# An mLSTM cell and a gated unit on one core: the order of Up's 64-row and 128-row products

## The chip, the cores and the metric

The kernel runs on one core of a Trainium2 chip. The time is the device time of one execution in microseconds (us); lower is better. A core has five engines with an instruction queue each: PE (TensorE, the matrix products; PEld is its loading of weights), DVE (VectorE), ACT (ScalarE), POOL (GpSimd) and SP (SyncE, which here only issues DMAs). They run side by side and wait for one another by semaphores.

## The reference, cut to what matters

Two blocks follow one another. The first is an mLSTM cell (4 batches, 8 heads, 768 steps, head dimension 40) that gives `attn_out`; the second is a gated unit with an input width of 320 and an inner width of 2048.

```python
x = attn_out.transpose(0, 2, 1, 3).reshape(B * S, H * D)   # 3072 x 320
h = x @ w_in                                               # "Up":   320 -> 2048
g = h * np.cos(h)                                          # the gate
out = g @ w_out                                            # "Down": 2048 -> 320
```

All values are float32. The recurrence of the first block is computed in chunks of steps, with one exponent matrix per head and chunk.

## The kernel before, in words

**Tiling.** The 768 steps are cut into 6 chunks of 128 (`NC`). A chunk of one batch is a *cell*, numbered n = 4 x chunk + batch, 24 in all. The tokens of one chunk, 4 batches x 128 steps = 512, are the moving columns of Up. The contraction of Up has 320 rows: two blocks of 128 (`NK`) and a rest of 64. The inner width 2048 is 16 blocks of 128, taken two at a time, e = 0 and 1, so a chunk has 8 pairs f2 = 0..7.

**Order.** The program is written out by hand; every engine executes its instructions in the order in which they are issued. `first_cells` does chunk 0 of the mLSTM block. Then `both_parts(c, b)` runs for every chunk c and every b in 0..3; it does the gated unit for chunk c, beside the cell n = 4(c + 1) + b of the chunk after it. In the last chunk (c = 5) no cell is left. Each `both_parts` has two half periods, i = 0 and i = 1, with one Up each, f2 = 2b + i.

**One Up** (class `Up`, L624 to L658) takes two PSUM banks from a pool of two (tag `up`), one for each e, and so needs both banks of the Up before to be free. Its constructor issues six products on PE: four with 128 rows (L636; block 0 for e = 0 and 1, then block 1 for both) and two with 64 rows (L639). In the last two, e = 0 uses rows 0 to 63 of the weights `w_in_l` and of x, and e = 1 uses rows 64 to 127, where a second copy of the same 64 rows of x stands. Each product of float32 appears in the trace as two records, two passes over the same 512 columns.

The chain behind it, for each e: `near` (L644, ACT) rounds h + 0.25 to an integer, `rest` (L647, DVE) takes the difference, `sin` (L652, ACT) is the sine of 2 pi times it, `gate` (L656, DVE) multiplies by h and writes g. `gate` is the last reader of the PSUM bank, so the next Up's first product into that bank waits for it.

**Around it on PE.** In half period i = 0 PE runs Up, `scores` (L482, 40 rows), Down's products, `values` (L508 to L517, 16 or 32 columns of weights), and in chunks 1 to 3 `seam` (L597, 40 columns of weights). In half period i = 1 it runs Up and then Down's products. From chunk 1 on, Down's products are those of a Strassen-like scheme (`products`, L717, and `run`, L743): from `sums` (L697, on DVE and POOL) of the g's, 12 or 14 per pair of blocks, handed out by `down_slot` (L786). At f2 = 1 of chunks 2 to 5 its place is taken by `late_products` of the chunk before (L737), followed by `combine_late`. `combine` (L755) adds the parts of the finished chunk on DVE and ACT after f2 = 0.

**Around it on the other engines**, in half period i = 1 of a cell: on ACT, two `near`, then two DMA issues of `seam_out` (L604, the 64 last rows of the next chunk's x, which wait for POOL's L538), then two `sin`; on DVE two `rest`, then `state` (L619, chunks 1 to 3 after POOL's `fade` L580), two `gate`, and the sums. `turn_blocks` (L455) makes the next cell's q and k on DVE, for `scores`. The 64 rows of x that Up's chunk c reads were written in chunk c - 1. At (chunk 1, f2 = 0) POOL also runs `weight_sums` (L692 to L695).

The calls of `both_parts` that matter here:

```python
for i in range(2):
    f2 = 2 * b + i
    up = Up(c, f2)
    ...
    for e in range(2):
        up.near(e)
    for e in range(2):
        up.rest(e)
    ...
    down_slot(c, f2)
```

Of the kernel before, what the change touches and what calls it, by code (L numbers as in the profile page):

```python
# [29 lines left out]
def kernel(  # L30
# [20 lines left out]
    nc = tc.nc  # L51
# [12 lines left out]
    NK = DM // 128  # L64
# [62 lines left out]
    w_in_sb = wp.tile([128, NK, DFF], FP, name="w_in_sb")  # L127

    w_in_l = wp.tile([128, NF // 2, 128], FP, name="w_in_l")
# [12 lines left out]
    def to_float32(dst, bits):  # L142
        take_apart(dst, bits)
        put_together(dst, bits)
# [166 lines left out]
    def sigmoid(c, bs=slice(0, B)):  # L311
        if c == 0:
            o = sig[c][:, bs]
            nc.scalar.activation(out=o, in_=o, func=AF.Sigmoid)
            return
        sig[c] = og
        K = C // 32
        nc.scalar.activation(out=sig[c][:, :, 0:2 * K], in_=raw_o[c][:, :, :, 0:32], func=AF.Sigmoid)
        for g in range(2):
            nc.scalar.activation(out=sig[c][:, :, 2 * K:3 * K, 16 * g:16 * g + 16:2],  # L320
                                 in_=raw_o[c][:, :, ts(g, K), 32:D], func=AF.Sigmoid)
# [7 lines left out]
    def load_two(n, which="qkKv"):  # L329
        c, b = divmod(n, B)  # L330
        m = n // 2 % 2
        for name, src in (("q", q), ("k", k)):
            if name in which:
                src = src.rearrange("b (p j) (c t a) d -> j c t (b p) (a d)", j=2, a=C // 32, t=32)
                for j in range(2):
                    for low in range(1 if n < 2 * B else 2):
                        x = 0 if low else 32
                        dst = raws[name][m][64 * j + 32 * low:64 * j + 32 * low + 32, x:x + WR]
                        nc.sync.dma_start(out=dst.rearrange("t (p x) -> t p x", x=C // 32 * D),
                                          in_=src[j, c, :, 4 * b:4 * b + 8])  # L340
        for name, dst, src in (("K", ks2[m], k), ("v", vs2[m], v)):
            if name in which:
                src = src.rearrange("b h (c t) d -> c t b h d", t=C)
                nc.sync.dma_start(out=dst[:, :, :, 0:D], in_=src[c, :, b:b + 2])
# [34 lines left out]
    def psum_o():  # L379
        return ps_o.tile([128, HP, C], FP, name="pm", tag="o")  # L380
# [6 lines left out]
    def decay_exponents(n):  # L387
        E = Es[n]
        if n < B:
            nc.vector.tensor_tensor(out=E, in0=E, in1=cols(n, 0, C), op=OP.subtract)  # L390
        nc.gpsimd.affine_select(out=E, in_=E, compare_op=OP.is_ge, fill=1.0e30, base=0,  # L391
                                pattern=[[0, H], [1, C]], channel_multiplier=-1)
# [45 lines left out]
    def clear_low():  # L438
        for w in "qk":
            nc.gpsimd.memset(raws[w][1], 0.0)  # L440
# [34 lines left out]
    def scores(n):  # L475
        pool, tag = psum(n)
        qT, kT = qkT[n]
        ps = [pool.tile([128, HP, C], FP, name="ps", tag=tag) for _ in range(2)]
        for p in range(HP):
            for j in range(2):  # L480
                r = slice(64 * j, 64 * j + D)
                nc.tensor.matmul(ps[j][:, p], kT[r, p], qT[r, p], start=True, stop=True)  # L482
        pss[n] = ps

    def weigh(n):
        for j in range(2):
            w = Es[n].rearrange("p (a j) t -> p a j t", j=2)[:, :, j]
            nc.vector.tensor_tensor(out=w, in0=pss[n][j], in1=w, op=OP.mult)  # L488
# [71 lines left out]
    def halves(n):  # L560
        for j in range(2):
            r = slice(64 * j, 64 * j + D)
            for lo, hi, x in ((0, 32, HP * 32 * j), (32, DV, H * 32)):
                s = st[n % B][r, x:x + HP * 32].rearrange("q (p d) -> q p d", p=HP)
                yield j, r, s if lo == 0 else s[:, :, 16 * j:16 * j + 16], slice(lo, hi)
# [58 lines left out]
    class Up:  # L624


        def __init__(self, c, f2):
            self.c, self.f2 = c, f2
            self.pu = [ps_u.tile([128, B * C], FP, name="pup", tag="up") for _ in range(2)]

            def x(i, r=slice(0, 128)):
                return xT[c][r, i].rearrange("p b t -> p (b t)")

            for i in range(NK):
                for e, pu in enumerate(self.pu):
                    nc.tensor.matmul(pu, w_in_sb[:, i, ts(2 * f2 + e, 128)], x(i), start=(i == 0), stop=False)  # L636
            for e, pu in enumerate(self.pu):
                r = slice(64 * e, 64 * e + 64)
                nc.tensor.matmul(pu, w_in_l[r, f2], x(NK, r), start=False, stop=True)  # L639
            self.n = [p3.tile([128, B * C], I32, name="n", tag="n") for _ in range(2)]  # L640


# [169 lines left out]
    def warm(k, bank=None):  # L812

        for _ in range(k):
            nc.tensor.matmul(bank or pw, nil, nil.unsqueeze(1).to_broadcast([128, HP, 128]), start=True, stop=True)
# [130 lines left out]
    def both_parts(c, b):  # L946

        n = (c + 1) * B + b
        cell = n < N
        for i in range(2):  # L950
            f2 = 2 * b + i
            up = Up(c, f2)
            if cell and i == 0:
                scores(n)
                if c == 0 and b == 0:

                    warm(8, psum_o())
            if cell and i == 1:
                if n % 2 == 1 and n > B + 1 and n + 3 < N:
                    load_two(n + 3, "Kv")  # L960
# [4 lines that stand above are left out]
            if i == 0:  # L965
                if cell:
                    weigh(n)
                    if n + 1 < N:
                        decay_exponents(n + 1)
                    if n == B:  # L970
                        clear_low()
                for e in range(2):
                    up.sin(e)
                    up.gate(e)
                if c > 0:
                    sums(c, f2)
                if b == 0 and 0 < c < NC - 1:
                    sigmoid(c + 1)

                if c == 0 and b > 0 and pieces:  # L980
                    to_float32(*pieces.pop(0))
                if c == 0:
                    next_out()
                if cell and n + 1 < N:
                    decay(n + 1)
            else:
                if cell:
                    seam_out(n)
                if pieces:
                    to_float32(*pieces.pop(0))  # L990
                if cell:
                    state(n)
                for e in range(2):
                    up.sin(e)
                    up.gate(e)
                if c > 0:
                    sums(c, f2)
                if n == B + 1:
                    low_dimensions(n + 1)
                while pieces:  # L1000
                    to_float32(*pieces.pop(0))
                if cell and n + 1 < N:
                    weigh_k(n + 1)
                    odd_values(n + 1)
            down_slot(c, f2)
            if (c, f2) == (1, 0):
                weight_sums(1)
            if cell and i == 0:
                turn_gate(n)
                values(n)  # L1010
                seam(n)
                normalize_turned(n)
                fade(n)
                if n % 2 == 1 and n > B + 1 and n + 3 < N:
                    load_two(n + 3, "qk")
                if n > B + 1 and n + 3 < N:
                    load_E(n + 3)
                if b == B - 2 and c + 2 < NC:
                    load_o(c + 2)
                if c == 0 and pieces:  # L1020
                    to_float32(*pieces.pop(0))
                sin_next()
            if f2 == 0 and c > 1:
                for p in range(2):
                    combine(c - 1, p)
            if i == 1:
                if c == 0 and b + 2 < B:
                    pieces.extend(weights_in(b + 2))
                    load_two((n + 3) // 2 * 2)
                    load_E(n + 3)  # L1030
                if cell and n + 1 < N:
                    turn_blocks(n + 1)
                    scale_q(n + 1)
                if c == 0:
                    next_out()
                if (c, f2) == (0, LAST):
                    weight_sums(0)
# [41 lines left out]
```

## Time and profile before

| what | value |
|---|---|
| three runs, us | 553.79, 556.17, 556.29 |
| median, us | 556.17 |
| span of the profiled execution, first to last instruction, us | 549.6 |
| the profiled execution's own time | not listed |
| mean granted clock of PE over the span | 0.981 |
| chain that ended last: share of PE | 65% |
| chain that ended last: DVE, ACT, POOL | 11%, 9%, 5% |
| Up's 128-row products, L636: records, busy us, mean ns | 384, 178.8, 609 |
| Up's 64-row products, L639: records, busy us, mean ns | 192, 54.2, 641 |

The page is of one execution, taken by the hardware profiler. "Busy" counts the time in which at least one instruction of the engine is under way. Matrix products overlap in the pipeline, so the mean length of one record is more than the distance from its start to the next start; two 64-row records run at the same time. What a product costs PE's stream is therefore read from start to start, and not from the length. The waits list gives the engine and line that waited, what released it, the total in us, the number of times and the longest. In a timeline, a figure in brackets is the engine's idle time before the instruction and what ended it. An engine's name with q (ACTq, SPq) stands for what its queue issues, such as DMAs.

### The profile page before, as it was taken

The page shows a single profiled execution, that of the slowest core. Times are in us where ns is not written, and L with a number is a line of the kernel's source. Part 1 is how long each engine was busy: PE and PEld are TensorE (multiplying, and loading weights), DVE is VectorE, ACT ScalarE, POOL GpSimd, SP SyncE. Part 2 cuts the span into 40 slices and gives each one's busy share as a digit, 9 for nine tenths or more (in the row PEclk, how much of TensorE's full clock was granted, in tenths as well). Part 3 has the DMA queues.
Part 4 walks back from the last instruction along what each step waited for, and adds up shares of the span by engine and source line. Part 5 has one row for each costly group of instructions (what it writes and reads, how often), then busy time and mean ns, then how long its engine had stood idle before and what let it go on. Part 6 is the DMA issues. An engine that isn't in the chain of part 4 may idle for free.

```text
span 549.6 us, 10494 instructions
## 1 busy us (share of the span) xinstructions
PE 522.2 (95%) x3844; PEld 348.6 (63%) x3844; DVE 420.0 (76%) x906; ACT 280.4 (51%) x537; POOL 235.3 (43%) x381
## 2 busy tenths in 40 slices
PE   7997989989979999999999999999999999999996
PEld 4873554546646666756766756766756757575755
DVE  5864999997877787887886888787887878674645
ACT  2867966847455445555535555535556533231311
POOL 7535456463784545534444435444423421221211
PEclk9968899999999999999999999999999999999999
DMA  9998878687926538318438428338410000010001
GB/s 135 228 201 224 244 163 215 137 188 186 163 92 155 72 92 187 41 67 202 49 93 183 44 67 199 52 92 181 47 69 25 5 6 6 1 48 1 1 1 48
DMA packets 99939, 57.81 MB, mean 105 GB/s; under 512 B 62304, under 2 KB 92608, under 8 KB 99888
## 3 DMA queue, kind: packets, MB, share of 16 engines
q1 hardware_dynamic: 96496, 55.64, 47.2%
q10 hardware_dynamic: 3248, 1.33, 1.1%
q8 instruction: 30, 0.49, 0.4%
q14 instruction: 21, 0.17, 0.1%
q0 software_dynamic: 144, 0.18, 0.1%
HBM read 51.71 MB, written 4.11 MB: 102 GB/s over the span
## 4 chain that ended last, share of the span: by engine, by line
PE 65%; DVE 11%; ACT 9%; POOL 5%; DMA 3%; issue 3%; SPq 3%; ACTq 0%; DVEq 0%; POOLq 0%
PE pup L636 24%; PE acc L746 21%; PE pup L639 7%; PE late L746 2%; PE ps L482 2%; DVE n L647 2%; ACT E L405 2%; DVE g L656 2%; PE vt L517 2%; PE po L668 2%; PE vt L508 1%; ACT n L644 1%; DMA E<-M_d 1%; DVE st L619 1%; DVE t L455 1%
## 5 line engine op out<-in xcount | busy, mean ns | idle before, releaser
L636 PE MATMUL pup<-xT,w_in_sb 128*128 128x512 f32 x384 | 178.8, 609 | 8.2 <-DVE g L656 7.8
L644 ACT ACTIVATE n<-pup 128x512 int32<-128x512 f32 x96 | 52.2, 595 | 206.4 <-PE pup L639 206.3
L647 DVE SCALAR_TENSOR_TENSOR n<-pup,n 128x512 f32<-128x512 f32 x96 | 61.8, 686 | 91.2 <-ACT n L644 91.2
L636 PEld LDWEIGHTS pup<-xT,w_in_sb 128*128 128x128 f32 x384 | 70.6, 192 | 84.2 <-issue 61.2
L710 POOL TENSOR_TENSOR D<-g 128x128 f32<-128x128 f32 x40 | 19.8, 495 | 178.6 <-DVE g L656 156.7
L652 ACT ACTIVATE n<-n 128x512 f32<-128x512 f32 x96 | 58.5, 631 | 18.5 <-DVE n L647 14.7
L656 DVE SCALAR_TENSOR_TENSOR g<-pup,n 128x512 f32<-128x512 f32 x96 | 61.7, 685 | 2.1 <-ACT n L652 0.4
L746 PE MATMUL acc<-w_out_sb,g 128*128 128x160 f32 x320 | 59.0, 305 | 0.0
L746 PE MATMUL acc<-T,g 128*128 128x160 f32 x320 | 58.3, 302 | 0.0
L639 PE MATMUL pup<-xT,w_in_l 64*128 64x512 f32 x192 | 54.2, 641 | 0.0
L746 PEld LDWEIGHTS acc<-w_out_sb,g 128*128 128x128 f32 x320 | 47.4, 190 | 6.8 <-issue 4.5
L746 PEld LDWEIGHTS acc<-T,g 128*128 128x128 f32 x320 | 47.8, 190 | 4.4 <-issue 3.8
L405 ACT ACTIVATE E<-E,tab 128x128 f32<-128x128 f32 x160 | 49.2, 391 | 2.0 <-POOL E L391 1.7
L668 PE MATMUL po<-w_out_sb,g 128*128 128x320 f32 x128 | 36.6, 439 | 3.8 <-POOL w_out_sb L162 3.7
L639 PEld LDWEIGHTS pup<-xT,w_in_l 64*128 64x128 f32 x192 | 14.4, 184 | 36.5 <-issue 34.3
L746 PE MATMUL acc<-T,S 128*128 128x160 f32 x160 | 35.3, 302 | 0.0
L538 POOL TENSOR_TENSOR yt<-yt,db 128x128 f32<-128x128 f32 x20 | 10.9, 545 | 55.0 <-DVE db L533 55.0
L668 PEld LDWEIGHTS po<-w_out_sb,g 128*128 128x128 f32 x128 | 23.7, 190 | 16.4 <-POOL w_out_sb L162 4.5
L482 PEld LDWEIGHTS ps<-t,t 40*128 40x128 f32 x384 | 24.8, 188 | 10.9 <-issue 8.0
L488 DVE TENSOR_TENSOR E<-ps,E 128x512 f32<-128x512 f32 x48 | 30.7, 681 | 0.0
L464 POOL TENSOR_TENSOR qG<-t,G 128x512 f32<-128x512 f32 x20 | 25.7, 1285 | 10.2 <-DVE t L455 10.0
L746 PE MATMUL acc<-w_out_sb,S 128*128 128x160 f32 x160 | 29.1, 301 | 0.0
(176 smaller groups left out, 902.5 us busy)
## 6 DMA issues: line engine op xcount, KB each, us to landing
E<-M_d SPq DMA_DIRECT2D x22, 512.0 KB
qr<-in_q_dram SPq DMA_DIRECT2D x36, 160.0 KB
kr<-in_k_dram SPq DMA_DIRECT2D x36, 160.0 KB
G<-G_d SPq DMA_DIRECT2D x20, 256.0 KB
bits<-in_moe_w_out_dram SPq DMA_DIRECT2D x8, 640.0 KB
bits<-in_moe_w_in_dram SPq DMA_DIRECT2D x32, 128.0 KB
out_dram<-o_sb SPq DMA_DIRECT2D x24, 160.0 KB
ks<-in_k_dram SPq DMA_DIRECT2D x10, 320.0 KB
```

What stands on the lines that cost most here:

```text
L405: nc.scalar.activation(out=Es[n][:, h], in_=Es[n][:, h], func=AF.Exp, scale=-1.0, bias=tab[:, c, 0, g:g + 1])
L464: nc.gpsimd.tensor_tensor(out=qG, in0=qkT[n][0], in1=Gs[n], op=OP.mult)
L482: nc.tensor.matmul(ps[j][:, p], kT[r, p], qT[r, p], start=True, stop=True)
L488: nc.vector.tensor_tensor(out=w, in0=pss[n][j], in1=w, op=OP.mult)
L636: nc.tensor.matmul(pu, w_in_sb[:, i, ts(2 * f2 + e, 128)], x(i), start=(i == 0), stop=False)
L639: nc.tensor.matmul(pu, w_in_l[r, f2], x(NK, r), start=False, stop=True)
L644: nc.scalar.activation(out=self.n[e], in_=self.pu[e], func=AF.Copy, bias=0.25)
L647: nc.vector.scalar_tensor_tensor(out=self.n[e].bitcast(FP), in0=self.pu[e], scalar=0.25, in1=self.n[e], op0=OP.add, op1=OP.subtract)
L652: nc.scalar.activation(out=r, in_=r, func=AF.Sin, scale=TWO_PI_DOWN)
L656: nc.vector.scalar_tensor_tensor(out=g, in0=self.pu[e], scalar=TWO_PI, in1=self.n[e].bitcast(FP), op0=OP.mult, op1=OP.mult)
L668: nc.tensor.matmul(po[c][b], gs[c, f][:, ts(b, C)], w_out_sb[:, f], start=(f == 0), stop=(f == NF - 1))
L746: nc.tensor.matmul(a, lhs, rhs, start=start, stop=stop)
```

## The change

`Up` gets a third argument. Where it is true, the two 64-row products are issued first and start the accumulation in PSUM, and the four 128-row products come behind them and end it. It is true in half period i = 1 of chunks 1 to 5, which is 20 of the 48 Ups. All the products, their operands and the number of instructions stay. Nothing else in the program is moved.

```diff
-        def __init__(self, c, f2):
+        def __init__(self, c, f2, low_first=False):
...
-            for i in range(NK):
+            def whole():
+                for i in range(NK):
+                    for e, pu in enumerate(self.pu):
+                        nc.tensor.matmul(pu, w_in_sb[:, i, ts(2 * f2 + e, 128)], x(i), start=(i == 0 and not low_first),
+                                         stop=(i == NK - 1 and low_first))
+
+            def halves():
                 for e, pu in enumerate(self.pu):
-                    nc.tensor.matmul(pu, w_in_sb[:, i, ts(2 * f2 + e, 128)], x(i), start=(i == 0), stop=False)
-            for e, pu in enumerate(self.pu):
-                r = slice(64 * e, 64 * e + 64)
-                nc.tensor.matmul(pu, w_in_l[r, f2], x(NK, r), start=False, stop=True)
+                    r = slice(64 * e, 64 * e + 64)
+                    nc.tensor.matmul(pu, w_in_l[r, f2], x(NK, r), start=low_first, stop=not low_first)
+
+            for part in (halves, whole) if low_first else (whole, halves):
+                part()
...
-            up = Up(c, f2)
+            up = Up(c, f2, c > 0 and i == 1)
```

## The prediction

> **What bounds the kernel.** I read the page's busy table first, then the waits of PE, then PE's timeline around one changed pair of Up.
>
> ```profile
> PE 522.2 (95%) x3844; PEld 348.6 (63%) x3844; DVE 420.0 (76%) x906; ACT 280.4 (51%) x537; POOL 235.3 (43%) x381
> ...
> PE pup L636 <- DVE g L656: 7.8, 6, 4.0
> ...
> PE late L746 <- DVE o_sb L763: 1.4, 3, 0.8
> ```
>
> PE is busy for 95% of the span, so what changes the length of PE's own stream changes the time. Its waits are few: six times Up's first product waited for `gate` of the Up before (7.8 us, 4.0 of it once), and three times `late` waited for `combine` (1.4 us). "Busy" hides a second loss, which the timeline shows. This is cell (chunk 3, i=1, f2=3); columns are start, length, engine and line.
>
> ```profile
> 338.57 0.54 PE L597 MATMUL pu<-vs,kw 128*40 128x48 f32 x16
> 339.04 3.70 PE L636 MATMUL pup<-xT,w_in_sb 128*128 128x512 f32 x8
> 342.67 1.13 PE L639 MATMUL pup<-xT,w_in_l 64*128 64x512 f32 x4
> 343.73 0.54 PE L746 MATMUL acc<-T,S 128*128 128x160 f32 x2
> 344.11 0.71 PE L746 MATMUL acc<-T,g 128*128 128x160 f32 x4
> 344.65 0.57 PE L746 MATMUL acc<-w_out_sb,S 128*128 128x160 f32 x3
> ```
>
> Call the 128-row products W (8 records per Up: 4 products in two passes), the 64-row ones H (4 records: two row halves side by side, two passes) and Down's products P. From start to start, single W records in mid-stream stand 0.429 us apart and P records 0.136. Eight W should take 3.43 us, but their stretch runs from 339.04 to 342.67, 3.63. Two H pairs should take 0.86 and take 1.06. The first two P take 0.38 (343.73 to 344.11) where the next four take 0.54, so 0.27 for two. Each stretch loses about 0.2. In the single records it falls at fixed places: at a change of shape the next record starts 0.09 late (W to H 0.523, H to P 0.519, where 0.429 is normal), and the second record of the new shape 0.10 late (W 0.533, H 0.527, P 0.240 for 0.136), since its weights were not loaded ahead. So **a change of shape costs 0.09 + 0.10 us**. Before, each i=1 Up in chunks 1 to 4 has three: narrow columns (`seam`'s 128x40, or in chunk 4 `values`' 128x32) to W, W to H, H to P.
>
> **The change, part by part.** No instruction is added or removed and no DMA moves; 20 of 48 Ups are reordered.
>
> *PE's stream, chunks 1 to 4.* From the last narrow product to the second P, before: 0.136 (to W) + 3.107 (eight W to the last) + 0.523 + 0.533 (H) + 0.519 + 0.240 = 5.06. After: 0.136 (to H, see below) + 0.533 + 0.519 (H to W, as H to P) + 3.107 + 0.429 (W to P, one shape) + 0.136 = 4.86. One change of shape goes: **0.20 us**.
>
> *Unknown: narrow columns to H.* No record shows it. The nearest are narrow columns to W (0.136, where 0.04 is the pace of these 48-column records: 0.096 late), `values` to `seam` (32 columns to 40: 0.203 for 0.109, 0.094 late) and `scores` to the 32-row transposes L273 (0.202 for 0.105: 0.097 late). All are near 0.096, and I take that. The ends: no loss at the entry (0.096 gained per Up) and a double one (0.096 lost), or 1.15 us either way over the 12 Ups that count. [...]
>
> *Chunk 5.* It has no cells, so P precedes Up. Before: W to H, H to P; after: P to H, H to W. Two and two, 0.
>
> *Where 0.20 does not count.* At f2=1 of chunks 2 to 4, P is `late`, which starts 0.92, 0.93 and 1.37 after the last H, waiting for `combine`; that queue does not depend on Up's order, so PE would only wait longer. At f2=1 of chunk 1 the next Up waits 4.2 us for `gate`: ACT's copies out wait for POOL's yt L538, which is queued behind `weight_sums`. The stalls behind them, in front of f2=2 (0.9, 0.9 and 0.2 us in chunks 2 to 4), stay for the same reason: near(0) starts 2.1 to 2.6 after the last H there, behind `combine`'s copy on ACT. These four Ups give 0. Twelve count: 12 x 0.203 = **2.44 us**.
>
> *The chain behind Up.* After H both banks finish together; after W, e=0's bank finishes two W (0.86 us) before e=1's. One stalled pair (chunk 1, f2=3 to 4):
>
> ```profile
> 179.01 1.13 PE L639 MATMUL pup<-xT,w_in_l 64*128 64x512 f32 x4
> ...
> 180.23 0.60 ACT L644 ACTIVATE n<-pup 128x512 int32<-128x512 f32 x1 [3.30 <-PE pup L639]
> 180.40 0.47 ACTq L604 DMA_DIRECT2D xT<-yt  x1
> ...
> 180.72 0.60 ACT L644 ACTIVATE n<-pup 128x512 int32<-128x512 f32 x1
> 180.86 1.29 DVE L647 SCALAR_TENSOR_TENSOR n<-pup,n 128x512 f32<-128x512 f32 x2 [2.33 <-ACT n L644]
> 180.91 0.61 ACTq L604 DMA_DIRECT2D xT<-yt  x1
> ...
> 181.59 1.23 ACT L652 ACTIVATE n<-n 128x512 f32<-128x512 f32 x2 [0.27 <-DVE n L647]
> ...
> 182.06 0.86 DVE L619 TENSOR_TENSOR st<-st,pu 40x128 f32<-40x128 f32 x4
> ...
> 182.96 1.29 DVE L656 SCALAR_TENSOR_TENSOR g<-pup,n 128x512 f32<-128x512 f32 x2
> 183.70 0.30 PEld L636 LDWEIGHTS pup<-xT,w_in_sb 128*128 128x128 f32 x2 [0.35 <-DVE g L656]
> ```
>
> Let T be the end of Up's last product (180.14). W at the end leaves T within 0.01 of where it was. Now `near(0)` starts at T+0.09 and `near(1)` follows it; after, near(0) is done and near(1) itself starts at T+0.09, so `rest(1)` starts where rest(0) did, T+0.72 for T+1.33: **0.61 earlier**. Behind it on DVE come `state` (0.86) and gate(0): T+2.21 for T+2.82. ACT's sin(0) may not gain: the two DMA issues (0.47 and 0.61) stand between near(1) and it on ACT, so it ends near T+2.0, still before T+2.21. Against PE, which is 0.20 earlier, the gate gains 0.41. The stall in front of the next Up (0.407 from the last P, 0.136 without; second W 0.533 for 0.429) is 0.27 + 0.10 = 0.375, and it goes: at chunk 1 f2=4 and 6 and chunk 2 f2=0, 3 x 0.375 = **1.13 us**. Elsewhere, but for f2=2, gate(0) ends 0.3 to 1.0 before the next Up. What is late next: `scores` after `turn_blocks` has 0.57 to 0.88 in hand there and `values` after `weigh` 1.07 or more, and both producers are on DVE, which moves up with the chain.
>
> *The tail.* Behind the last Up, the 41st P record waits for DVE's sums (L708): it starts 0.337 after the 40th (0.136 normally), and its follower at 0.240. In chunk 5 there is no `state`, and gate(1) ends 0.54 earlier after T (the second rest 0.61 earlier, then sin and gate), while T comes 0.20 later against P, since H no longer lies between W and P. So the chain gains about 0.34, more than the 0.20 it lacks, and 0.20 + 0.10 = **0.30 us** goes.
>
> *A new wait.* H needs both banks at once, W the second 0.86 later. In 19 of the 20 the gates are done at least 0.9 us ahead; at chunk 5, f2=1 gate(1) ends at 476.56 and PE arrives at 476.48 (476.39 + 0.09): with 0.05 to wake, 0.13 is lost, the W behind it waiting too.
>
> Sum: 2.44 + 1.13 + 0.30 - 0.13 = 3.74 us, of a span of 549.6, so 545.9. The profiled execution's own time is not listed; the three runs are 553.79, 556.17 and 556.29, so 4.2 to 6.7 us lie outside the span or in the spread. On the median: 556.17 - 3.74 = **552.4 us**, 0.67% less.
>
> **Rivals.**
> 1. *Only PE's stream gains.* If the chain stays as late as it is (sin(0), held by ACT's DMA issues, taking DVE's place as the last), the three stalls stay and also swallow their Ups' 0.20: 3.74 - 1.13 - 0.61 = 2.0 saved, 554.2. For it: the issues end at 181.52, only 0.07 before sin(0). Against: DVE's `state` ends after sin(0) anyway.
> 2. *The halves no longer run side by side.* In all 48 Ups the two H of a pair start 6 to 7 ns apart, but always behind W. If behind narrow columns they ran one after the other, each Up would take 2 x 0.429 = 0.86 more: 12 x (0.86 - 0.20) = 7.9 more, less 1.4 for stalls and tail, so 6.5 slower, 562.7. It decides from 0.31 us per Up (3.74 / 12). Against: `scores`' pairs start 7 ns apart too.
> 3. *The clock.* The 4.3 us without products before chunk 1, f2=2 is followed by 3.5 us at a granted clock of 0.53, where five W took 3.84 for 2.15: 1.7 lost. PE will idle 0.2 longer there. One such stretch more gives 2.0 saved (554.1), none gives 5.4 (550.7). [...]
> 4. *Nothing comes through:* another wait takes up the gain, 556.2. DVE's 76% and the slacks above speak against it.
>
> **How the numbers follow.** Forecast 0.66, rivals 0.16, 0.06, 0.06 (half each way) and 0.06, in the order 1, 2, 3, 4. A measurement tells about 0.5% (2.8 us) from no change. Faster by more: 0.66, less 0.04 for the dear entry (2.6 saved), plus 0.03 of rival 3: 0.65. Same: 0.04 + 0.16 + 0.03 + 0.06 = 0.29. Slower: 0.06. The forecast with both ends of the unknown entry is 551.3 to 553.6. The range runs from 550.0 (the sum taken from the lowest run, 553.79) to 555.2 (rival 1 and a microsecond of spread between runs); rivals 2 and 4, 0.12, are outside.
>
> **What would show it.** H pairs 7 ns apart, then W 0.519 later, P 0.429 after the last W and 0.136 after the first P; narrow to H near 0.136; the stalls in front of chunk 1 f2=4, 6 and chunk 2 f2=0 gone and rest(1) at T+0.72. H pairs 0.43 apart, or gate(0) still near T+2.8, would make it wrong.

## The result and the profile after

| what | before | changed |
|---|---|---|
| first comparison, median us (runs) | 556.07 (4) | 548.51 (4) |
| ratio, 95% interval | | 0.9892 [0.9861, 0.9922] |
| second comparison, all on one chip, median us (runs) | 554.09 (23) | 551.00 (6) |
| ratio, 95% interval | | 0.9936 [0.9910, 0.9961] |
| span of the first, second profiled execution | 549.6, 552.9 | 546.9, 549.5 |
| of it from the first product of (1,3) to the end | 374.3, 374.7 | 371.3, 371.0 |

(1,3) stands for chunk 1, f2 = 3, here and below. The ratios are estimates with their intervals, and not quotients of the two medians. The kernel became faster, by 0.6% to 1.1%. Executions of one kernel lie up to 5 us apart (before: 551.2 to 556.5), and the last row shows where: from (1,3) to the end two executions of a kernel agree within 0.5 us, while the part ahead of it, which the change hardly touches, took 175.4 to 178.4 us in the four profiles of the two kernels. So I measure the change from (1,3) on, where it saves **3.0 to 3.7 us**. That is the 3.1 us of the second comparison's medians; the 7.6 us of the first, with four runs each, I put down in part to the spread of the part ahead, which its unprofiled runs can't show. 1.7 to 1.9 us of every execution whose span is listed lie outside the span, so the first profile of before was one of its shorter executions.

The page and PE's waits after the change:

```profile
PE 518.9 (95%) x3844; PEld 349.2 (64%) x3844; DVE 421.9 (77%) x906; ACT 280.5 (51%) x537; POOL 235.0 (43%) x381
...
PE pup L637 <- DVE g L663: 8.1, 6, 4.2
...
PE late L753 <- DVE o_sb L770: 1.4, 3, 0.8
```

PE is 3.3 us less busy for the same 3844 records. The line of its waits for gate is no smaller; 4.2 of it is the wait in front of (1,2), which the change leaves, and one more is told of at e4. How much of the gain is PE's stream and how much its stalls can't be read from these lines; e5 and e6 tell it. PE's timeline in (3,3), the cell that the prediction showed, with one of PEld's weight loads:

```profile
337.16 0.54 PE L597 MATMUL pu<-vs,kw 128*40 128x48 f32 x16
337.63 1.13 PE L643 MATMUL pup<-xT,w_in_l 64*128 64x512 f32 x4
338.69 0.30 PEld L637 LDWEIGHTS pup<-xT,w_in_sb 128*128 128x128 f32 x2 [0.76 <-issue]
338.69 3.70 PE L637 MATMUL pup<-xT,w_in_sb 128*128 128x512 f32 x8
342.23 0.43 PE L753 MATMUL acc<-T,S 128*128 128x160 f32 x2
342.50 0.71 PE L753 MATMUL acc<-T,g 128*128 128x160 f32 x4
```

H now takes 1.06 (337.63 to 338.69), W 3.54 and the first two P 0.27. Before, the stretches were 3.63, 1.06 and 0.38: together 0.20 more. In the single records, H to W is 0.519, the last W to P 0.429 and the next P 0.136. The entry that no row had shown, narrow columns to H, is 0.136, just what W had there (0.203 behind chunk 4's `values`, which W had too).

The chain behind Up in (1,3), where before had a stall:

```profile
179.61 0.60 ACT L651 ACTIVATE n<-pup 128x512 int32<-128x512 f32 x1 [2.47 <-PE pup L637]
...
180.24 1.49 DVE L654 SCALAR_TENSOR_TENSOR n<-pup,n 128x512 f32<-128x512 f32 x2 [1.47 <-ACT n L651]
180.41 0.60 ACT L651 ACTIVATE n<-pup 128x512 int32<-128x512 f32 x1 [0.20 <-PE pup L637]
180.47 1.12 ACTq L604 DMA_DIRECT2D xT<-yt  x2
...
181.64 1.15 ACT L659 ACTIVATE n<-n 128x512 f32<-128x512 f32 x2 [0.63 <-issue]
181.65 0.86 DVE L619 TENSOR_TENSOR st<-st,pu 40x128 f32<-40x128 f32 x4
...
182.54 1.29 DVE L663 SCALAR_TENSOR_TENSOR g<-pup,n 128x512 f32<-128x512 f32 x2
...
183.47 1.02 PE L637 MATMUL pup<-xT,w_in_sb 128*128 128x512 f32 x2
```

T, the end of Up's last product, is 180.37. near(0) now starts 0.76 ahead of T and the second rest at T+0.67 (T+1.33 before), gate at T+2.17 (T+2.82). The next Up's W no longer shows idle time in front of it: it starts 0.136 after the last P. But sin has not moved much: ACT stands idle 0.63 behind the two DMA issues.

### The profile page after: what moved, and what is told of

It is laid out like the page before. It is cut to its first block, busy times and chain, and to the rows that moved or that the text cites. A ratio compares the mean times of both kernels' runs of the same rounds, so it can differ in the third digit from the quotient of the medians.

```text
span 546.9 us, 10494 instructions
## 1 busy us (share of the span) xinstructions
PE 518.9 (95%) x3844; PEld 349.2 (64%) x3844; DVE 421.9 (77%) x906; ACT 280.5 (51%) x537; POOL 235.0 (43%) x381
## 3 DMA queue, kind: packets, MB, share of 16 engines
q10 hardware_dynamic: 3248, 1.33, 1.2%
## 4 chain that ended last, share of the span: by engine, by line
PE 67%; DVE 10%; ACT 6%; POOL 5%; DMA 5%; issue 3%; SPq 3%; ACTq 0%; DVEq 0%; POOLq 0%
PE pup L637 25%; PE acc L753 21%; PE pup L643 7%; PE late L753 2%; PE ps L482 2%; PE po L675 2%; DVE n L654 2%; PE vt L517 2%; DVE g L663 1%; PE vt L508 1%; ACT E L405 1%; DMA bits<-in_moe_w_out_dram 1%; DMA E<-M_d 1%; DVE t L455 1%; PE pu L597 1%
## 5 line engine op out<-in xcount | busy, mean ns | idle before, releaser
L651 ACT ACTIVATE n<-pup 128x512 int32<-128x512 f32 x96 | 53.8, 595 | 198.7 <-PE pup L643 138.2
L654 DVE SCALAR_TENSOR_TENSOR n<-pup,n 128x512 f32<-128x512 f32 x96 | 63.2, 687 | 85.5 <-ACT n L651 83.9
L717 POOL TENSOR_TENSOR D<-g 128x128 f32<-128x128 f32 x40 | 19.7, 493 | 175.6 <-DVE g L663 154.4
L675 PE MATMUL po<-w_out_sb,g 128*128 128x320 f32 x128 | 38.0, 452 | 3.8 <-POOL w_out_sb L162 3.7
```

The source lines that it names most:

```text
L651: nc.scalar.activation(out=self.n[e], in_=self.pu[e], func=AF.Copy, bias=0.25)
L654: nc.vector.scalar_tensor_tensor(out=self.n[e].bitcast(FP), in0=self.pu[e], scalar=0.25, in1=self.n[e], op0=OP.add, op1=OP.subtract)
L675: nc.tensor.matmul(po[c][b], gs[c, f][:, ts(b, C)], w_out_sb[:, f], start=(f == 0), stop=(f == NF - 1))
```

## The experiments

"From (1,3)" is the time from that Up's first product to the end of the span. A *hold* is a stall in front of (1,6) that is longer than the same kernel's stalls in front of (1,4) and (2,0); where it comes from is told at e4. The profiles are from several chips, but from (1,3) on they can be compared: less its hold, the kernel before takes 374.2 to 374.3 in its two profiles and in e10, whose change lies ahead of (1,3).

**e1 and e2: both kernels again.** No edit.

> The unchanged kernel once more, timed against itself. Two things are to be told apart. Theory A: what the change itself saves is what the two profiles show, 2.7 us of span (549.6 to 546.9), and the profiled execution of before was one of its shorter ones, so that the spans of other executions of before are 552 to 554.5 (its times of 553.8 to 556.3, less the 1.8 us that lie outside the span in the runs of the changed kernel); the lost time should then sit in parts that the change doesn't touch (the loads and the first chunk), and would differ from run to run. Rival B: the unchanged kernel always takes 552 us or more of span except under that one profile, and loses it in the changed region (chunks 1 to 5); a new profile would then show 3 to 5 us more than the first one from chunk 1 on. Under both, the ratio to itself is 1.000 within 0.003.

> The changed kernel once more, on the same chip as the others. Theory A: ratio to before between 0.986 and 0.995, span 546 to 549 us, the profile again 2.7 to 3.5 us shorter than before's from chunk 1 to the end, and the stall in front of chunk 1 f2=6 either there (0.7 us between products) or gone (0.14), by whether ACT's second DMA issue of the cell before took 1.6 or 0.6 us. Rival B: the stall there is fixed, and the ratio repeats at 0.989.

Measured: e1 0.9999 [0.9979, 1.0020], from (1,3) 374.7; e2 0.9936 [0.9910, 0.9961], from (1,3) 371.0. The new profile of before is 3.3 us longer than the first, and 2.8 of that is ahead of (1,3) (178.2 against 175.4). That speaks for theory A, but not all of it lies where A put it: 1.8 is ahead of chunk 1, 1.0 in the stretch from (1,2) to (1,3), and the rest is a hold. e2's new profile differs from the first one of the changed kernel likewise: 178.4 against 175.6 ahead, 0.2 less behind. Three details of e2's expectation were missed: its span of 549.5 is above the 549 given, it is 4.0 shorter than e1 from the start of chunk 1 on, where at most 3.5 was given, and the stall in front of (1,6) is 0.47, neither of the two values.

A part of the spread can be named. In the nine profiles with the long stall in front of (1,2), the stretch (1,2) to (1,3) took 12.9 us three times and 13.5 to 14.1 six times; in it PE's granted clock was 0.53 over 3.5 us in the first profile of before and 0.59 in that of the changed kernel, both with 12.9 (see e10). The times also go with the clock granted over the whole execution: of the 23 of before on this chip, the five at 0.969 took 555.25 to 556.53, the ten at 0.978 took 553.11 to 554.45, and the one at 0.984 took 551.25. The changed kernel's three at 0.978 took 549.97 to 551.23, about 3 us less than before's ten. In the first comparison the changed kernel's four had 0.978 to 0.986; those of before are not on record, so how much of its 7.6 us goes with the clock is not shown.

**e3: no head start, by a swapped order on ACT and DVE.**

```diff
-            for e in range(2):
+            both = (1, 0) if c > 0 and i == 1 else (0, 1)
+            for e in both:
                 up.near(e)
-            for e in range(2):
+            for e in both:
                 up.rest(e)
```

> The change, but in the reordered Ups near and rest take e=1 first and e=0 second, so that the chain behind Up gets no head start from the earlier bank: rest's second starts at T+1.33 again instead of T+0.67. It takes the chain's part of the gain away and leaves PE's. Theory (the gain is the sum of both): PE's stream still saves 0.20 in 9 Ups, the three stalls in front of chunk 1 f2=4, 6 and chunk 2 f2=0 come back at 0.4 to 0.5 us between products and swallow the other three, and the tail's stall grows by 0.2: span 1.2 to 1.8 us under before in the parts from chunk 1 on, 1.3 to 2 us over the changed kernel. Rival (PE's stream alone gives all of it): the same as the changed kernel within 0.5 us.

Measured: 1.0002 [0.9982, 1.0022], from (1,3) 374.8: the whole gain gone, more than expected. The edit does more than I meant. rest(0) is now second, so sin(0) waits for it (T+2.05), and in chunks 4 and 5, without state, gate(0) starts at T+2.71, where before had T+2.11. New waits follow: (4,1) to (4,2) takes 10.76 for 10.19, (4,4) to (4,5) and (4,6) to (4,7) each take 0.27 more, and from (5,7) to the end it takes 19.45 for 18.77. It shows that the chain matters, but not how much; e5 does that.

**e5: the same PE stream, with e = 0's bank done last.** Then near(0) waits for T, and near(1) stands behind it as before.

```diff
             def whole():
                 for i in range(NK):
-                    for e, pu in enumerate(self.pu):
+                    for e, pu in list(enumerate(self.pu))[::-1 if low_first else 1]:
```

> The change, but in the reordered Ups each block's 128-row product of e=1 comes ahead of that of e=0, so that the bank of e=0, for which near waits first, is the one that is done last. PE's stream is that of the changed kernel, and the chain behind Up is again that of before (near(0) at T+0.09, second rest at T+1.33, gate(0) at T+2.82 with state and T+2.11 without). Measured from the first product of chunk 1 f2=3 to the end of the span (before 374.3 and 374.7 in two profiles, the changed kernel 371.3 and 371.0). Theory (the gain is the sum of PE's stream and the chain): 9 Ups save 0.20, three are swallowed by the stalls in front of chunk 1 f2=4, 6 and chunk 2 f2=0, which stay at 0.6; the tail loses 0.2 and chunk 5 f2=1 0.1, and some second products come 0.04 late: 1.0 to 1.6 saved against before, 372.9 to 373.5. Rival (PE's stream gives all, the chain nothing): 371.0 to 371.5. Rival (the chain gives all): 374.3 or more.

Measured: 0.9970 [0.9945, 0.9996], from (1,3) 373.0, without a hold: 1.2 saved against before's 374.3, as expected. The timeline in (1,3), T = 182.46:

```profile
182.56 0.60 ACT L651 ACTIVATE n<-pup 128x512 int32<-128x512 f32 x1 [3.32 <-PE pup L637]
...
183.06 0.59 ACT L651 ACTIVATE n<-pup 128x512 int32<-128x512 f32 x1
...
185.29 1.29 DVE L663 SCALAR_TENSOR_TENSOR g<-pup,n 128x512 f32<-128x512 f32 x2
...
186.04 0.70 PE L637 MATMUL pup<-xT,w_in_sb 128*128 128x512 f32 x1 [0.32 <-DVE g L663]
```

Both near follow T again, gate starts at T+2.83, and the next Up waits for it. (1,3) to (1,4) takes 8.33, exactly as before the change, though PE's stream in it is 0.20 shorter: the stall swallows it. Where no stall stands, as from (2,3) to (2,4), it takes 8.40 for 8.60.

**e6: the chain's part alone.** The 64-row products stand between the two blocks: three changes of shape as before, but e = 0's bank done first.

```diff
...
+            whole(0)
+            if low_first:
+                halves()
+            whole(1)
+            if not low_first:
+                halves()
```

> In the 20 reordered Ups the 64-row products stand between block 0's and block 1's 128-row products. PE's stream then has as many changes of shape as before (narrow to W, W to H, H to W; none from W to P), and e=0's bank is done 0.86 us ahead of e=1's, as in the changed kernel. It keeps the chain's part alone. From the first product of chunk 1 f2=3 to the end (before 374.3 and 374.7, changed 371.3 and 371.0). Theory (sum of both): the three stalls go, 1.13, and 0.2 in the tail: 1.2 to 1.5 saved, 372.8 to 373.4; the time from one Up to the next stays 8.60 in chunks 2 to 4. Rival (the chain gives all): 371.0 to 371.5. Rival (chain nothing): 374.3 or more.

Measured: 0.9975 [0.9950, 0.9999], from (1,3) 373.3, with a hold of 0.48 (the stall in front of (1,6) is 0.38 longer than none, and the second product 0.10 late); without it 372.8, so 1.4 saved, as expected. PE's timeline in (3,3):

```profile
341.06 0.54 PE L597 MATMUL pu<-vs,kw 128*40 128x48 f32 x16
341.53 1.98 PE L636 MATMUL pup<-xT,w_in_sb 128*128 128x512 f32 x4
343.44 1.13 PE L642 MATMUL pup<-xT,w_in_l 64*128 64x512 f32 x4
344.50 1.98 PE L636 MATMUL pup<-xT,w_in_sb 128*128 128x512 f32 x4
346.32 0.43 PE L756 MATMUL acc<-T,S 128*128 128x160 f32 x2
346.60 0.57 PE L756 MATMUL acc<-T,g 128*128 128x160 f32 x3
```

From the last narrow group to the second group of P it takes 5.54; in before's profile 5.54 too (338.57 to 344.11), in the changed kernel 5.34. So the middle position saves PE nothing, and the stalls in front of (1,4) and (2,0) are gone all the same.

**e8: only the Ups that were counted at nothing.**

```diff
-            up = Up(c, f2, c > 0 and i == 1)
+            up = Up(c, f2, c > 0 and i == 1 and (b == 0 or c == NC - 1))
```

> The new order only in the eight Ups that the prediction counted at nothing for PE's stream: f2=1 of chunks 1 to 4, and the four of chunk 5. From the first product of chunk 1 f2=3 to the end (before 374.3 and 374.7, changed 371.3 and 371.0). Theory: f2=1 gives 0 (late waits for combine, the next Up for gate), chunk 5 f2=1 loses 0.13, the tail gains 0.2 to 0.3: 374.1 to 374.6. Rival (each Up saves 0.2, wherever it stands): 8 x 0.2 = 1.6 saved, 372.7 to 373.1.

Measured: 1.0004 [0.9981, 1.0028], from (1,3) 374.6, with a hold of 0.52, so 374.1 without: 0.2 saved in eight reordered Ups. f2 = 1 of chunks 2 to 4 gives nothing ((2,1) to (2,2) takes 10.43, before 10.44). In chunk 5 the two terms are visible: (5,1) loses 0.11, and the tail gains 0.30 (from (5,7) to the end it is 0.39, but (5,7) itself begins 0.09 later, as H behind P starts 0.09 later than W behind P did).

**e4: the DMA issues behind the sines.**

```diff
-                if cell:
+                if cell and c == 0:
                     seam_out(n)
...
                 for e in range(2):
                     up.sin(e)
                     up.gate(e)
+                if cell and c > 0:
+                    seam_out(n)
```

> The change, and from chunk 1 on the two DMA issues of seam_out stand behind the sines on ACT instead of between near and sin. Theory (the one stall that the changed kernel has left in front of chunk 1 f2=6 comes from ACT's second DMA issue, 1.58 us there): sin(0) starts near T+0.7 in all cells, that stall goes (0.7 to 0.14 between products), and the span is 0.6 us under an execution of the changed kernel that has the stall, and equal to one without it; in chunk 4, without state, gate(0) starts at T+1.4 instead of T+1.94, which nothing waits for. Rival (the wait is for something else, such as rest or state): the stall stays. A loss is possible if the later landing of the 64 rows delays the next chunk's first Up; not expected, as they have over 8 us.

Measured: 0.9927 [0.9901, 0.9953], from (1,3) 370.5, which is 0.5 to 0.7 under the changed kernel. The times alone don't tell the two apart; the traces do. First the changed kernel in (1,5), T = 199.30:

```profile
199.34 0.60 ACT L651 ACTIVATE n<-pup 128x512 int32<-128x512 f32 x1 [0.20 <-PE pup L637]
199.40 2.11 ACTq L604 DMA_DIRECT2D xT<-yt  x2
...
201.56 1.15 ACT L659 ACTIVATE n<-n 128x512 f32<-128x512 f32 x2 [1.62 <-DMA xT<-yt]
202.22 1.29 DVE L663 SCALAR_TENSOR_TENSOR g<-pup,n 128x512 f32<-128x512 f32 x2 [0.78 <-ACT n L659]
```

The issues take 2.11 us on ACT's queue here, not 1.12, and sin waits behind them until T+2.26; DVE, done with state, stands idle 0.78 for it. That is the hold: PE's next W comes 0.705 after the last P. Then e4 in the same place, T = 202.55:

```profile
203.15 0.63 ACT L659 ACTIVATE n<-n 128x512 f32<-128x512 f32 x1
...
204.01 1.12 ACTq L604 DMA_DIRECT2D xT<-yt  x2
204.72 1.29 DVE L663 SCALAR_TENSOR_TENSOR g<-pup,n 128x512 f32<-128x512 f32 x2
```

sin(0) starts at T+0.60, gate at T+2.17, and the next W 0.136 after the last P. A hold at (1,6) is in both profiles of the changed kernel, and in e1, e6, e8 and e10; all of them issue the DMAs ahead of sin. In these six the second issue in (1,5) took 1.33 to 1.93 us, and the stall, 0.47 to 1.04 from product to product, is always 0.85 to 0.89 shorter than it: the longer the issue, the longer the hold. The first profile of before and e5 have 0.61 there and no hold; e3 has 1.15 and none, since its sin waits for rest until T+2.05 anyway.

The long issue is not peculiar to that cell. In all nine profiles that issue ahead of sin, the second issue in (4,1) is long too (0.78 to 1.59), in the first profile of before 1.56, but nothing on PE waits for it there. In e4, e7 and e9, which issue behind the sines from chunk 1 on, none takes over 0.65. What makes an issue long stays open: SP issues DMAs of its own beside the long ones, but also beside those of 0.61 in (2,1) and (3,1).

**e7: an attempt at the big stall, with too much moved.** In both kernels PE idles over 4 us (4.0 and 4.2) in front of (1,2), because gate waits for what stands behind weight_sums on POOL. On top of e4:

```diff
-            if (c, f2) == (1, 0):
-                weight_sums(1)
+            if c == 1 and f2 < 4:
+                weight_sum(f2)
...
-                if cell:
+                if cell and c == 0:
                     state(n)
...
                 if cell and c > 0:
                     seam_out(n)
+                    state(n)
```

(`weight_sum(j)` is the j-th of weight_sums' four operations, on the same operands.)

> A version meant to beat both: the change, with seam_out and state behind the gates from chunk 1 on, and POOL's four weight_sums operations (6.3 us in a row at chunk 1, f2=0) handed out one to each half period of chunk 1, f2=0 to 3. In before and after, PE idles 4.3 to 4.5 us in front of chunk 1 f2=2, since gate there waits for what stands behind those operations on POOL, and the products after it run for some us at half the clock (12.9 to 14.1 us from that Up to the next, where such a period elsewhere in the chunk takes 11.2). Theory: the stall goes to under 0.5 us, and the slow clock with it: 4 us plus 1.7 to 2.9, so 5 to 7 us under the changed kernel, ratio to before 0.980 to 0.985. Rival: POOL is then late with its sums or with yt later in chunk 1, and Down's products or Up wait there: 1 to 4 us under the changed kernel.

Measured: 0.9981 [0.9955, 1.0007]. The stall in front of (1,2) fell from 4.5 to 1.0, but from (1,3) it took 376.5, 5.9 more than e4. The rival had the kind of loss right, a new wait in the cells, but with another culprit than POOL's weight sums, and the loss is larger than it said: it put e7 1 to 4 us under the changed kernel, and e7's ratio is above the changed kernel's. `scores` waited for turn_blocks 6.4 us in all. PE's wait, and from the timeline in (1,6) DVE's last sum beside POOL's kw:

```profile
PE ps L482 <- DVE t L455: 6.4, 6, 2.0
...
200.83 1.09 POOL L410 TENSOR_TENSOR kw<-ks,tab 128x512 f32<-128x512 f32 x1
200.94 1.12 DVE L723 TENSOR_TENSOR g<-g 128x128 f32<-128x128 f32 x1
```

In eleven of the twelve cells with state it took 1.12 to 1.13 us there; in e4 and e9, where kw comes later and not beside it, 0.28. In the rows above DVE's operation begins 0.11 behind POOL's and ends 0.14 behind it; what makes it take longer there is not shown.

**e9: e7 with state back in its place.** e4, and weight_sums handed out as in e7.

> The version of e7 without its moved state: the change, ACT's DMA issues behind the sines, and the four weight_sums operations handed out one to each half period of chunk 1, f2=0 to 3; state stays between rest and the sines. In e7 the stall in front of chunk 1 f2=2 went (4.3 to 1.0), but scores then waited 0.5 to 2.6 us for turn_blocks in each cell: DVE's last sum took 1.12 us instead of 0.28 there, beside POOL's kw of 1.09. Theory (moving state brought the two engines' work on top of each other): with state back, scores wait as little as in the changed kernel (0.42 after the last H, but 0.7 at f2=2 of chunks 2 and 3), gate in chunk 1 f2=1 starts 3 to 4.3 us earlier than in the changed kernel, the slow clock behind it goes: from chunk 1 f2=1 to f2=3 20.5 to 22 us (changed 25.1 to 25.9), and from there to the end 370.5 to 371.5; ratio to before 0.983 to 0.988. Rival (the spread weight_sums themselves make turn_blocks late): scores still waits about 1 us in chunk 1 f2=2 and 4, ratio 0.988 to 0.993.

Measured: **0.9833 [0.9803, 0.9864]**, 544.78 us (6 runs) against 554.70 (12 runs) of before on the same chip. From (1,1) to (1,3) it takes 20.7 us (changed kernel 25.1 and 25.9), and from (1,3) 370.5, the same as e4. e9 differs from e7 in the place of state alone, so it was the moved state that made scores wait. Its ratio is below that of either comparison of the changed kernel, though the two were not timed side by side.

**e10: before, with the handed-out weight_sums alone.** The edit is the first part of e7's on the kernel before.

> The kernel before with nothing but the four weight_sums operations handed out one to each half period of chunk 1, f2=0 to 3. It shows how much of e9 is the stall's, without the change. Theory: from chunk 1 f2=1 to f2=3 20.5 to 22 us (before 25.1 to 26.2), from there to the end 374 to 375 as before; ratio to before 0.990 to 0.994. If the change and the stall are independent, e9's gain is this one's and 3.2 to 4 us of the change's.

Measured: 0.9915 [0.9884, 0.9945], (1,1) to (1,3) 20.6, from (1,3) 374.9 with a hold. This and e4 multiply to 0.9915 x 0.9927 = 0.984, near e9's 0.983, so the two gains add up. Two windows of 3.5 us, the slow one behind the stall in the changed kernel and then the one behind the shorter stall in e9 (columns: window, its length, busy us of PE, PEld, DVE, ACT, POOL, PE's granted clock, DMA share, GB/s):

```profile
164.10:167.60 3.50, 3.50 (x6) 1.31 (x5) 2.64 (x4) 0.00 (x0) 3.42 (x5) 0.59 0.34 101
```

```profile
161.30:164.80 3.50, 3.46 (x8) 1.43 (x8) 3.40 (x7) 0.00 (x0) 2.62 (x5) 1.00 0.04 13
```

The stalls are 4.5 us and 1.8 us from product to product. The window behind the long one has a granted clock of 0.59, the one behind the short one 1.00. So I estimate that a third to a half of what the shorter stall gains comes with the clock: the stall shrinks by 2.8 us, and the products behind it, from (1,2) to (1,3), take 11.2 instead of 12.9 or 13.7.

## Why the prediction was right, point by point

**The direction and the size of the sum were right.** It said 3.74 us; from (1,3) on, where all its terms lie, the changed kernel saves 3.0 in the first pair of profiles and 3.7 in the second. Without holds on either side it is 3.7: the changed kernel's two profiles, less holds of 0.67 and 0.44 (the longer stall and the 0.10 of the second product behind it), give 370.6, and so does e4 (370.5), against before's 374.3. So the forecast of 3.74 holds for an execution of the changed kernel without a hold, and neither profile of it was one. The predicted 552.4 us lies 1.4 above the second comparison's median and 3.9 above the first one's, whose median of 548.5 is under the range. The spread between executions, 5 us, was wider than the three runs had shown, and the range too narrow for it. The prediction's remark that 4.2 to 6.7 us lie "outside the span or in the spread" was mostly spread: outside are 1.8.

**PE's stream, 12 x 0.203.** Right to the record: every spacing that was forecast appears. From (2,0) to (5,0), with 9 of the 12 Ups, before takes 245.73 and the changed kernel 243.84: 1.89, where 9 x 0.203 and 0.10 for the second W of (2,0) are 1.93. The prediction put the second record's 0.10 to weights that were not loaded ahead. The rows place this one record earlier: at 338.69 the first weight load of the new shape begins together with its product, after PEld stood idle 0.76, where in mid-stream a load begins 0.43 ahead. The second load begins 0.11 behind the first and 0.43 ahead of its own product, as far as any W's.

**The unknown entry.** 0.136, the middle of the three cases: the first record comes 0.096 late, and the second 0.10. So the entry costs what the other changes cost, about 0.20 (in (3,3) the first two records are 0.09 and 0.10 late at W to H before and at H to W now); what makes a change cost that is not shown.

**What counts for nothing.** Right: e8 gives 0.2 in eight Ups, which is the tail's 0.30 less the 0.11 at (5,1).

**The chain, 1.13 for three stalls.** The mechanism was right and the size too large in the executions that were profiled. The second rest starts 0.66 earlier (0.61 forecast) and two of three stalls are gone, (1,4) and (2,0), at 0.375 each. The third, at (1,6), is still there, 0.71 from product to product in one profile and 0.47 in the other. It is what rival 1 named, ACT's DMA issues ahead of sin(0), but in one of the three cells only, where an issue takes 1.58 or 1.33 instead of 0.61 us. In the first profile of before, on which the prediction rests, no issue in these three cells was that long; in e1's there is one, with the stall 0.48 longer. But that first profile has an issue of 1.56 in (4,1): the prediction took the 0.47 and 0.61 of one cell as fixed, though the same trace has an issue that takes longer.

**The new wait at (5,1) and the tail.** 0.11 lost (0.13 forecast) and 0.30 gained (0.30). In the changed kernel's (5,1) the two halves start 0.12 apart instead of 0.007.

**The two parts.** e5 (PE's stream without the chain) saves 1.2 and e6 (the chain without the stream) 1.4; together 2.7, while both at once save 3.7. The missing 1.0 is the 0.20 of the three stalled Ups, which is worth nothing while gate is late (0.6 in all), and in e5 six second products 0.04 late (0.24) and a tail that is 0.20 longer than before's. The prediction had this in rival 1, where the stalls "also swallow their Ups' 0.20".

**The rivals.** 2 (halves one behind the other) fell: the pairs start 7 ns apart behind narrow columns too. 3 (the clock) shows as spread: the stretch from (1,2) to (1,3), with its granted clock of 0.53 and 0.59 over 3.5 us in the first profile of each kernel, took 12.9 and 13.9 us in the two profiles of before, 12.9 and 13.7 in those of the changed kernel, so it is no part of the difference. 4 fell.

## What to carry to other kernels

On an engine that is busy all the time, count the changes of product shape and not only the products: here each change in the rows or columns of the weights on the way into W, H or P cost 0.20 us (W to H 0.52 and 0.53, where 0.43 is normal), while from P to W in chunk 5, which differ in the moving columns alone, it cost nothing (W 0.136 behind the last P, the next W 0.429 behind it). Putting the odd shape next to another odd shape removed one change. Ask of every saving what the next instruction waits for: three of the twelve cells would have gained nothing without the earlier gate. When two executions differ by more than the effect, find a landmark in the trace behind the part that varies, and measure from there.

## What the runs showed of the hardware that I had not expected

- A DMA issue of `seam_out` in ACT's instruction stream took 0.47 to 0.65 us in 463 of 480 cases over the twelve profiles, and 0.72 to 1.93 in the other 17. sin, which stands behind it on ACT, started only when it was done, 0.05 us behind its end in the changed kernel's (1,3) and (1,5) (told at e4).
- At the changes between W, H and P, PEld stood idle 0.76 us, and the first weight load of the new shape began only with its product; the first two records came 0.09 and 0.10 us late ((3,3), both kernels).
- A DVE sum of 0.28 us (e4 and e9) took 1.12 to 1.13 beside a POOL product of 1.09 us, in eleven of twelve cells (e7).
